# One ring of eight PSUM banks for layers three and four, and one tile for queries and values

## The chip, the cores and the metric

The kernel runs on one core of a Trainium2 chip. The metric is the device time of one execution in microseconds (us), lower is better. Engines are named as in the profile: PE is TensorE's matmul, PEld its weight load, DVE is VectorE, ACT is ScalarE, POOL is GpSimd, SP is SyncE, which issues all DMAs here.

## The reference

Two batches of eight heads, 768 positions, head size 64, all in float32. Attention over a window of 16 positions and over 24 block summaries gives a 1536 x 512 matrix `x`; two dense blocks follow.

```python
k_sum = k.reshape(B, H, nb, 32, D).max(axis=3); v_sum = v.reshape(B, H, nb, 32, D).mean(axis=3)
a = softmax(concat([where(|i - j| < 16, q k^T / 8, -1e9), q k_sum^T / 8 + log(32)]))
x = (a @ concat([v, v_sum])).transpose(...)                 # 1536 x 512
h = np.maximum(np.maximum(x @ w1, x @ w2), x @ w3)           # 1536 x 768  (layer one)
y = h @ moe_w_out                                            # 1536 x 512  (layer two)
out = ((y @ w_a) * (y @ w_b)) @ moe2_w_out                   # 1536 x 1536 (three), 1536 x 512 (four)
```

## The kernel before

The tokens are cut into four chunks of 384 (two to a batch). Attention is made group by group (a chunk and a pair of heads): queries `q_t` (four tiles taken in turn) and values `v_t` (one tile for each pair of heads) are loaded into SBUF, scores go to `ps`, transposed weights to `pst`, results to `psv`. Layers one and two (`layers12`) multiply weights by `x`, into PSUM tiles `ph` and `py`. Every float32 product is made of three fp32r matmuls (`mm3`: high by high, low by high, high by low part).

Layer three (`layer3`) is a seven-product scheme after Strassen and Winograd. For each of six pairs of column blocks `n` there is one pass of kind "a" and one of kind "b", and in a pass 7 products times two batches `b`. A product is 6 matmuls of 384 columns. The seven products of a batch use three PSUM banks, by the table `PRODUCTS`: products 0, 2, 4 and 6 add into bank `qb`, products 1 and 5 into bank `qg`, product 3 into `qd`. After each product the bank is read: products 0, 1 and 2 are copied by ACT (L626: `s`, `m`, `u`), 3, 4 and 5 are added to such a copy by DVE (L636 in kind "a", L642 in kind "b"), product 6 is read by ACT in kind "a" (L634) and by DVE in kind "b" (L640). So the read of product 6 is the last of `qb`, the read of product 5 the last of `qg`. Kind "b" goes on: POOL or DVE multiplies by the result of kind "a", and ACT and DVE split the product into `hg` (L514, L515).

Layer four (`layer4`) makes 12 output tiles for each `n`, 6 matmuls of 512 columns each into a bank `po`, three for each of two `hg`; ACT copies (`n` = 0) or DVE adds (L683) the bank to `acc`, which is stored at the last `n`. The order of the passes is a0, b0, a1, o0, b1, a2, o1 and so on (o is layer four); in the first and in the last pass of layer three all of batch 0 comes before batch 1.

Every PSUM tile belongs to a tag with a number of buffers. Before, `qb`, `qg` and `qd` have two each, and `po` shares the pair of tag `m` with layers one and two. The planner that builds the program places each tile in a bank, with no more tiles alive of a tag than its buffers, and orders the instructions of PE, ACT, DVE and POOL by its own cost model; each engine then runs its list in order. A tile in a bank that another held before waits for the last read of the other. SP's list stays in the order of the program text.

The weights of all layers come as 60 raw blocks (`w64`, 512 KB each, numbered q from 0) and are turned into float32 by ACT, DVE and POOL (`w_round`, L439 to L447), then split (`w_parts`, L451, L452). Blocks 0 to 7 have eight buffers of their own, blocks 8 to 23 (layers one and two) share `W64[0]` buffers, blocks 24 to 59 share `W64[1]` = 3. How far loads are written ahead of use depends on the same numbers:

```python
ahead = min(AHEAD[0] + 2 * (w_done < ERA0 + 4), W64[w_done + AHEAD[0] > N12] - 2 * (w_done >= ERA0 + 4))
```

with `AHEAD[0]` = 4, `ERA0` = 8, `N12` = 24, and `w_done` the count of blocks finished.

Of the kernel before, what the change touches and what calls it, by code (L numbers as in the profile page):

```python
# [9 lines left out]
F32 = mybir.dt.float32  # L10
# [8 lines left out]
B, H, S, D = 2, 8, 768, 64  # L19
P = 128  # L20
# [5 lines left out]
NP = H // 2  # L26
HALF = 64
WIN = HALF + 2 * WINDOW
NC = WIN + NB
# [7 lines left out]
NCH, MAXT = len(CHUNKS), max(SIZES)  # L37
# [5 lines left out]
N1, N2, NK = 3 * FF1 // P, FF1 // P, FF2 // P // 3  # L43
# [9 lines left out]

W64, W32, WBUFS, QB, FB, SM, GB, BANKS = (6, 3), (4, 3), (24, 10), 4, (9, 1), 2, (12, 9), (2, 2, 1, 2, 2)

GATE, ROOM, SUMS, EARLY34 = (2, 3), 16, (46, 48, 50, 52), 6
LEAD, TURN, ERA0, ASKS, AHEAD, PRE, TURNS = 5, (11, 2, 2), 8, (3, 4, 5, 7, 9), (4, 1), 3, ((6, N1 - 6, 6, 4, 4, 8, N1 - 8, 4, 12), (24, 34), (34, 44))

# [10 lines left out]
def attention_then_maxout_then_bilinear(ctx: ExitStack, tc: tile.TileContext, qt, kt, vt, vwin, wall, const, out):  # L77
# [6 lines left out]
    one = ctx.enter_context(tc.tile_pool(name="one", bufs=1))  # L84
# [14 lines left out]
    ps_m = ctx.enter_context(tc.tile_pool(name="ps_m", bufs=BANKS[3], space=PSUM))  # L99
# [9 lines left out]
    cst = take(C_ALL)  # L109
    ident = cst[:, C_ID:C_ID + P]  # L110

    q_t = [one.tile([P, MAXT, 2, P], F32, name=f"q{i}") for i in range(QB)]

    k_t = [take(NSEG * SEG) for _ in range(NP)]

    v_t = [one.tile([NC, MAXT, 2, 2, D], F32, name=f"v{p}") for p in range(NP)]
    VSEG, v_s = 2 * SIZES[0] + 1, {}


# [8 lines left out]
    marks, raw = {}, {}  # L130
# [3 lines left out]
    @contextmanager  # L134
    def behind_all(*names):

        with ExitStack() as held:
            for name in names:
                if name in marks:
                    held.enter_context(tc.issue_after(marks[name]))  # L140
            yield

    @contextmanager
    def chain(on=True):

        with behind_all("pe") if on else ExitStack():
            yield
# [89 lines left out]
    def scores(g, i):  # L237

        c, p = groups[g]
        t, q = CHUNKS[c][1] + i, q_t[g % QB]  # L240
        if i == 0:
            exps[g] = (sm_p.tile([P, MAXT, 2, NC], F32, tag="s", name="s"),
                       sm_p.tile([P, MAXT, 2], F32, tag="sm", name="sm"))
        s, sm = (x[:, i] for x in exps[g])
        ps = ps_s.tile([P, 2, NC], F32, tag="s", name="ps")
        nm = sm_p.tile([P, 2], F32, tag="nm", name="nm", bufs=4)
        with chain(g <= NP) if g <= NP else behind_all("first"):
            for a in range(2):
                k0 = (2 * t + a) * SEG + HALF - Z_AT[a]
                ins = T.matmul(ps[:, a], q[:, i, a], k_t[p][:, k0:k0 + NC], start=True, stop=True).ins  # L250
            if g <= NP:
                marks["pe"] = ins
        for a in range(2):
            mask = cst[:, MASK[t, a]:MASK[t, a] + NC]

            marks["scores", g, i] = V.tensor_tensor_reduce(s[:, a], ps[:, a], mask, -1.0 / D ** 0.5, 3e38, ALU.add, ALU.min, nm[:, a:a + 1]).ins  # L256
            A.activation(s[:, a], s[:, a], AF.Exp, bias=nm[:, a:a + 1], scale=-1.0, accum_out=sm[:, a:a + 1])  # L257
        if g <= NP:
            turn_over(TURN[1 + p // 2])
# [54 lines left out]
    def opening():  # L314

        def spread_(p, i):
            with behind_all(("scores", min(p + 1, NP - 1), i)):
                spread(0, p, raw["v", p])
# [178 lines left out]
    def flush():  # L497
        while late:
            late.pop(0)()

    def bank(name):

        return ps_m.tile([P, 512], F32, tag="m", name=name)
# [4 lines left out]
    def mm3(ps, w, o, x, first, last, more=False):  # L508

        for n, (i, j) in enumerate(((0, 0), (1, 0), (0, 1))):  # L510
            T.matmul(ps, w[:, i, o:o + P], x[:, j], start=first and n == 0, stop=last and n == 2, skip_group_check=more)  # L511

    def split(dst, src, eng):
        A.activation(dst[:, 0], src, AF.Copy)  # L514
        eng.tensor_tensor(dst[:, 1], src, dst[:, 0], ALU.subtract)  # L515
# [86 lines left out]
    def half(tag):  # L602
        return mo_p.tile([P, MAXT * P], F32, tag=tag, name=tag, bufs={"ca": 9, "t": 3}.get(tag, 2))

    def layer3(kind, n, cs):

        nonlocal w_freed
        ws = w_t[kind, n]
        ps, kept = {}, {}
        each = [(i, b) for i in range(7) for b in range(B)]  # L610
        if (kind, n) in (order34[0], order34[-2]):
            each.sort(key=lambda x: x[1])
        for i, b in each:
            w, y, bank_ = PRODUCTS[i]
            first = (b, bank_) not in ps
            if first:
                ps[b, bank_] = ps_m.tile([P, 512], F32, tag=f"q{bank_}", name=f"q{bank_}")[:, 0:MAXT * P]
            (wt, o), to = ws[w], ps[b, bank_]
            for k in range(2):
                mm3(to, wt, o + k * P, ops[b, y][:, :, k], first and k == 0, k == 1, not first)  # L620
            flush()

            def evac(i=i, b=b, to=to):
                def keep(name):
                    kept[b, name] = t = half(name)
                    A.activation(t, to, AF.Copy)  # L626

                def result(f, j, x):

                    c = 2 * b + j  # L630
                    if kind == "a":
                        cs[c, f] = t = half("ca")
                        if x is None:
                            A.activation(t, to, AF.Copy)  # L634
                        else:
                            V.tensor_tensor(t, to, x, ALU.add)  # L636
                        return
                    t = half("t")
                    if x is None:
                        V.tensor_tensor(t, to, cs[c, f], ALU.mult)  # L640
                    else:
                        V.tensor_tensor(t, to, x, ALU.add)  # L642
                        G.tensor_tensor(t, t, cs[c, f], ALU.mult)  # L643
                    gs[n, c, f] = g = hg_p.tile([P, 2, MAXT * P], F32R, tag="g", name="hg", bufs=GB[1])
                    split(g, t, V)

                if i in (0, 1, 2):
                    keep(("s1", "m5", "u2")[i])
                elif i == 3:
                    result(0, 0, kept[b, "s1"])  # L650
                elif i == 4:
                    result(1, 1, kept[b, "m5"])
                elif i == 5:
                    result(0, 1, kept[b, "u2"])
                else:
                    result(1, 0, None)

            late.append(evac)
            yield
        w_freed += 3  # L660
# [3 lines left out]
    def layer4(n, q):  # L664
        nonlocal w_freed
        for c in range(NCH):
            for i in range(CHUNKS[c][2]):
                ps = bank("po")
                for f in range(2):
                    w, g = w_t[q + f], gs[n, c, f][:, :, i * P:(i + 1) * P]  # L670
                    T.matmul(ps, g[:, 0], w[:, 0], start=(f == 0), stop=False)  # L671
                    T.matmul(ps, g[:, 0], w[:, 1], start=False, stop=False)  # L672
                    T.matmul(ps, g[:, 1], w[:, 0], start=False, stop=(f == 1))  # L673
                flush()

                def evac(c=c, i=i, ps=ps):
                    if n == 0:
                        if not acc:
                            sums = acc_p.tile([P, NCH, MAXT, DM], F32, tag="acc", name="acc", bufs=1)
                            acc.update({(c, i): sums[:, c, i] for c in range(NCH) for i in range(MAXT)})  # L680
                        A.activation(acc[c, i], ps, AF.Copy)
                    else:
                        V.tensor_tensor(acc[c, i], ps, acc[c, i], ALU.add)  # L683
                    if n == NG - 1:
                        r0 = (CHUNKS[c][0] * NT + CHUNKS[c][1] + i) * P
                        nc.sync.dma_start(out=out[r0:r0 + P, :], in_=acc[c, i])

                late.append(evac)
                yield
        w_freed += 2  # L690

    def layers34():
        q, cas = N12, {}
        for kind, n in order34:
            if kind == "o":
                flush()
                yield from layer4(n, q)
            else:
                yield from layer3(kind, n, cas.setdefault(n, {}))
            q += 2  # L700
# [99 lines left out]
```

## Time and profile before

| what | value |
|---|---|
| time, median of 3 runs | 561.99 us (561.78 to 562.42) |
| the profiled execution's own time | 562.49 us |
| its span, first to last instruction | 560.7 us |
| PE busy | 545.3 us, 97% of the span |
| DVE, ACT, POOL busy | 377.3, 279.2, 201.6 us |
| mean granted TensorE clock | 0.996 |

The profiled execution lies 0.5 us above the median; 1.8 us of its time lie outside the span. PE busy counts modelled ends of pipelined matmuls, so a busy PE is no proof of a PE at its peak; the idle times before its instructions are what can be won back.

### The profile page before, as it was taken

What the parts mean: (1) busy time and instruction counts of PE and PEld (TensorE: products, weight loads), DVE (VectorE), ACT (ScalarE), POOL (GpSimd) and SP (SyncE); (2) the same over time, 40 slices, a digit from 0 to 9 for tenths busy, and PEclk for the clock granted to TensorE, in tenths of its full rate; (3) what the DMA queues carried; (4) which work ended last, traced back from release to release, by engine and by line L of the source; (5) the groups of instructions that cost most, each with busy time, mean ns of one, the idle gap of its engine ahead of it and who ended that gap; (6) DMA issues with size and microseconds to landing.
All of it is one profiled execution on the core that took longest, in us unless ns stands there. A gap on an engine that the chain in (4) does not pass through costs nothing.

```text
span 560.7 us, 9032 instructions
## 1 busy us (share of the span) xinstructions
PE 545.3 (97%) x3374; PEld 516.3 (92%) x3374; DVE 377.3 (67%) x790; ACT 279.2 (50%) x672; POOL 201.6 (36%) x177
## 2 busy tenths in 40 slices
PE   8899999999999999999997999999999999999997
PEld 8889999999999999999997999999889989999985
DVE  5798966875323622739869756866967987773374
ACT  4799765766532413625675656534535443341220
POOL 3479997632010111513504322513412332220030
PEclk9999999999999999999999999999999999999999
DMA  8995244573000030313302222112023121000005
GB/s 302 367 304 227 79 150 147 180 221 100 22 1 1 2 111 3 113 38 114 113 0 77 75 76 75 44 69 85 29 76 113 37 77 38 1 0 1 1 33 192
DMA packets 16987, 51.81 MB, mean 92 GB/s; under 512 B 2096, under 2 KB 2480, under 8 KB 16944
## 3 DMA queue, kind: packets, MB, share of 16 engines
q1 hardware_dynamic: 16944, 51.25, 26.8%
q8 instruction: 26, 0.43, 0.3%
q14 instruction: 17, 0.14, 0.1%
HBM read 48.09 MB, written 3.15 MB: 91 GB/s over the span
## 4 chain that ended last, share of the span: by engine, by line
PE 79%; DVE 10%; DMA 5%; ACT 3%; issue 1%; POOL 1%; SPq 0%; ACTq 0%; DVEq 0%; POOLq 0%
PE ph L511 27%; PE qb L511 13%; PE py L511 9%; PE qg L511 6%; PE po L673 5%; PE po L672 5%; PE po L671 5%; PE ps L250 3%; PE qd L511 3%; DMA w<-wall 2%; DVE wt L452 2%; PE psv L305 2%; DVE hg L515 2%; PE pst L286 2%; DVE t L642 2%
## 5 line engine op out<-in xcount | busy, mean ns | idle before, releaser
L511 PE MATMUL ph<-x,wt 128*128 128x384 f32 x864 | 157.4, 337 | 0.0
L511 PEld LDWEIGHTS ph<-x,wt 128*128 128x128 f32 x864 | 149.0, 188 | 0.3
L447 POOL TENSOR_TENSOR w<-w,w 128x512 int32<-128x512 int32 x60 | 82.6, 1382 | 152.8 <-DVE w L446 90.1
L511 PE MATMUL qb<-yt,wt 128*128 128x384 f32 x576 | 113.9, 338 | 5.2 <-DVE t L642 3.1
L511 PEld LDWEIGHTS qb<-yt,wt 128*128 128x128 f32 x576 | 101.9, 188 | 10.7 <-DVE t L642 3.5
L514 ACT ACTIVATE hg<-t 128x384 fp32r<-128x384 f32 x72 | 37.0, 522 | 80.7 <-POOL t L643 34.3
L643 POOL TENSOR_TENSOR t<-t,ca 128x384 f32<-128x384 f32 x36 | 43.0, 1206 | 85.9 <-DVE t L642 85.9
L683 DVE TENSOR_TENSOR acc<-po,acc 128x512 f32<-128x512 f32 x60 | 40.8, 686 | 27.9 <-PE po L673 27.8
L511 PE MATMUL qg<-yt,wt 128*128 128x384 f32 x288 | 58.7, 340 | 0.5 <-DVE t L642 0.5
L671 PE MATMUL po<-wt,hg 128*128 128x512 f32 x144 | 56.2, 390 | 0.5 <-ACT hg L514 0.5
L672 PE MATMUL po<-wt,hg 128*128 128x512 f32 x144 | 56.7, 394 | 0.0
L673 PE MATMUL po<-wt,hg 128*128 128x512 f32 x144 | 56.2, 396 | 0.1
L511 PE MATMUL py<-hg,wt 128*128 128x384 f32 x288 | 54.7, 339 | 0.0
L511 PEld LDWEIGHTS qg<-yt,wt 128*128 128x128 f32 x288 | 51.9, 192 | 2.4 <-DVE t L642 0.8
L538 DVE TENSOR_TENSOR t<-ph,t 128x384 f32<-128x384 f32 x48 | 26.5, 554 | 37.3 <-PE ph L511 29.1
L511 PEld LDWEIGHTS py<-hg,wt 128*128 128x128 f32 x288 | 49.5, 188 | 0.2
L257 ACT ACTIVATE s<-s,nm 128x120 f32<-128x120 f32 x96 | 37.2, 392 | 22.1 <-DVE nm L256 21.7
L451 ACT ACTIVATE wt<-w 128x512 fp32r<-128x512 f32 (+1 forms) x60 | 35.1, 586 | 24.7 <-PE qb L511 15.3
L452 DVE TENSOR_TENSOR wt<-w,wt 128x512 fp32r<-128x512 f32 (+1 forms) x44 | 32.9, 748 | 18.6 <-ACT wt L451 18.5
L515 POOL TENSOR_TENSOR hg<-t,hg 128x384 fp32r<-128x384 f32 x24 | 26.8, 1121 | 46.4 <-ACT hg L514 46.4
L515 DVE TENSOR_TENSOR hg<-t,hg 128x384 fp32r<-128x384 f32 x48 | 40.8, 860 | 3.6 <-ACT hg L514 3.5
L443 ACT ACTIVATE w<-w 128x512 int32<-128x512 uint32 x60 | 39.0, 667 | 0.0
(80 smaller groups left out, 780.6 us busy)
## 6 DMA issues: line engine op xcount, KB each, us to landing
w<-wall SPq DMA_DIRECT2D x60, 512.0 KB, 3.4
q<-qt SPq DMA_DIRECT2D x15, 384.0 KB, 6.6
row<-kt SPq DMA_DIRECT2D x8, 416.0 KB, 5.0
full<-vt SPq DMA_DIRECT2D x8, 384.0 KB, 6.4
out<-acc SPq DMA_DIRECT2D x12, 256.0 KB, 2.0
v<-vwin SPq DMA_DIRECT2D x12, 192.0 KB, 6.0
v<-vwin SPq DMA_DIRECT2D x12, 96.0 KB, 5.6
q<-qt SPq DMA_DIRECT2D x1, 256.0 KB, 4.3
```

Source lines behind the costliest of these rows:

```text
L257: A.activation(s[:, a], s[:, a], AF.Exp, bias=nm[:, a:a + 1], scale=-1.0, accum_out=sm[:, a:a + 1])
L443: A.activation(lw.bitcast(I32), lw, AF.Copy, scale=2.0 ** -29)
L447: G.tensor_tensor(w.bitcast(I32), w.bitcast(I32), lw.bitcast(I32), ALU.add)
L452: eng.tensor_tensor(w[:, 1], r, w[:, 0], ALU.subtract)
L511: T.matmul(ps, w[:, i, o:o + P], x[:, j], start=first and n == 0, stop=last and n == 2, skip_group_check=more)
L514: A.activation(dst[:, 0], src, AF.Copy)
L515: eng.tensor_tensor(dst[:, 1], src, dst[:, 0], ALU.subtract)
L643: G.tensor_tensor(t, t, cs[c, f], ALU.mult)
L671: T.matmul(ps, g[:, 0], w[:, 0], start=(f == 0), stop=False)
L672: T.matmul(ps, g[:, 0], w[:, 1], start=False, stop=False)
L673: T.matmul(ps, g[:, 1], w[:, 0], start=False, stop=(f == 1))
L683: V.tensor_tensor(acc[c, i], ps, acc[c, i], ALU.add)
```

## The change

Layer three's three pairs and layer four's share of tag `m` become one tag `r` with eight buffers, so any of the tiles `qb`, `qg`, `qd` and `po` may take any free one of eight. The tag `m` keeps its pair for layers one and two. Queries and values become slices of one SBUF tile `held`. The buffers of weight blocks 8 to 23 go from six to four, which by the line quoted above also changes how far ahead these loads are written: from 6 to 4 blocks while `w_done` is under 12, and from 4 to 2 for `w_done` 12 to 20. The rename in `behind_all` has no effect on the program.

```diff
-W64, W32, WBUFS, QB, FB, SM, GB, BANKS = (6, 3), (4, 3), (24, 10), 4, (9, 1), 2, (12, 9), (2, 2, 1, 2, 2)
+W64, W32, WBUFS, QB, FB, SM, GB, BANKS = (4, 3), (4, 3), (24, 10), 4, (9, 1), 2, (12, 9), (2, 2, 1, 2, 2)
-LEAD, TURN, ERA0, ASKS, AHEAD, PRE, TURNS = 5, (11, 2, 2), 8, ...
+RING, LEAD, TURN, ERA0, ASKS, AHEAD, PRE, TURNS = 8, 5, (11, 2, 2), 8, ...
-    q_t = [one.tile([P, MAXT, 2, P], F32, name=f"q{i}") for i in range(QB)]
+    held = one.tile([P, QB + NP, MAXT, 2, P], F32, name="qv")
+    q_t = [held[:, i] for i in range(QB)]
-    v_t = [one.tile([NC, MAXT, 2, 2, D], F32, name=f"v{p}") for p in range(NP)]
+    v_t = [held[0:NC, QB + p].rearrange("k i a (h d) -> k i a h d", h=2) for p in range(NP)]
-        with ExitStack() as held:
+        with ExitStack() as pins:
-                ps[b, bank_] = ps_m.tile([P, 512], F32, tag=f"q{bank_}", name=f"q{bank_}")[:, 0:MAXT * P]
+                ps[b, bank_] = ps_m.tile([P, 512], F32, tag="r", name=f"q{bank_}", bufs=RING)[:, 0:MAXT * P]
-                ps = bank("po")
+                ps = ps_m.tile([P, 512], F32, tag="r", name="po", bufs=RING)
```

## Rows read from the trace of the kernel before

**Rows 1.** The page: busy time of each engine, its share, instructions.
```profile
PE 545.3 (97%) x3374; PEld 516.3 (92%) x3374; DVE 377.3 (67%) x790; ACT 279.2 (50%) x672; POOL 201.6 (36%) x177
```

**Rows 2.** Waits of PE alone: us in total, times, longest.
```profile
PE qb L511 <- DVE t L642: 3.1, 1, 3.1
...
PE qb L511 <- DVE t L640: 1.0, 3, 0.6
...
PE qb L511 <- ACT u L626: 0.6, 1, 0.6
PE qg L511 <- DVE t L642: 0.5, 1, 0.5
PE po L671 <- ACT hg L514: 0.5, 1, 0.5
PE qb L511 <- ACT s L626: 0.5, 1, 0.5
```

**Rows 3.** A window of 20 us: busy PE, PEld, DVE, ACT, POOL, PEclk, DMA share, GB/s.
```profile
300.00:320.00 20.00, 16.75 (x85) 15.81 (x84) 18.91 (x28) 12.46 (x25) 10.37 (x8) 0.91 0.28 98
```

**Rows 4.** Timeline around the longest wait: start, us, engine, instruction, [idle before <-releaser].
```profile
301.40 2.24 PE L511 MATMUL qb<-yt,wt 128*128 128x384 f32 x12
...
306.19 0.55 DVE L642 TENSOR_TENSOR t<-qb,m 128x384 f32<-128x384 f32 x1
306.65 0.54 DVE L642 TENSOR_TENSOR t<-qg,u 128x384 f32<-128x384 f32 x1
...
306.78 1.86 PE L511 MATMUL qb<-yt,wt 128*128 128x384 f32 x6 [3.14 <-DVE t L642]
```

**Rows 5.** Windows at that place, columns as in the window above.
```profile
303.50:306.70 3.20, 0.15 (x1) 0.00 (x0) 3.20 (x9) 2.59 (x5) 0.00 (x0) 1.00 0.04 12
...
307.40:310.60 3.20, 3.20 (x11) 3.20 (x11) 3.20 (x4) 1.36 (x3) 3.20 (x3) 0.50 0.24 60
```

**Rows 6.** Timeline of PE: two of four instructions that waited for a last read.
```profile
405.18 1.32 PE L511 MATMUL qb<-yt,wt 128*128 128x384 f32 x6 [0.57 <-DVE t L640]
451.57 1.34 PE L511 MATMUL qg<-yt,wt 128*128 128x384 f32 x6 [0.51 <-DVE t L642]
```

**Rows 7.** By tile, po: ns min/median/max, first and last start.
```profile
L671 PE MATMUL po<-wt,hg x144: 387/389/504, 287.9 to 556.0; 128*128 128x512 f32 x144
...
L681 ACT ACTIVATE acc<-po x12: 581/592/602, 317.9 to 348.5; 128x512 f32<-128x512 f32 x12
```

**Rows 8.** By tile, qd: the same columns.
```profile
L511 PE MATMUL qd<-yt,wt x144: 333/334/343, 244.9 to 508.7; 128*128 128x384 f32 x144
...
L642 DVE TENSOR_TENSOR t<-qd,s x12: 542/550/558, 269.8 to 539.8; 128x384 f32<-128x384 f32 x12
```

**Rows 9.** SP's timeline: issues of weight blocks 17 to 23, then of batch 1.
```profile
64.28 19.82 SPq L421 DMA_DIRECT2D w<-wall  x7
...
94.75 0.34 SPq L173 DMA_DIRECT2D full<-vt  x1
...
104.38 0.52 SPq L173 DMA_DIRECT2D full<-vt  x1
```

**Rows 10.** DMA issues of the weights: count, KB each, median us to landing.
```profile
w<-wall SPq DMA_DIRECT2D x60, 512.0 KB, 3.4
```

**Rows 11.** By line, L439: DVE's first step on every third early block, last on 22.
```profile
L439 DVE TENSOR_SCALAR psw<-w x8: 673/683/686, 28.3 to 98.7; 128x512 f32<-128x512 f32 x8
```

**Rows 12.** ACT's timeline: the first step on block 23.
```profile
101.36 0.62 ACT L441 ACTIVATE psw<-w 128x512 f32<-128x512 f32 x1
```

**Rows 13.** PE's timeline where layer two begins.
```profile
131.43 1.20 PE L511 MATMUL py<-hg,wt 128*128 128x384 f32 x6
```

**Rows 14.** The end, timeline: DVE's last read of a bank.
```profile
556.87 0.69 DVE L683 TENSOR_TENSOR acc<-po,acc 128x512 f32<-128x512 f32 x1 [0.67 <-PE po L673]
```

**Rows 15.** SP's timeline: a part of the tile `kept`, which also holds the keys.
```profile
3.54 0.43 SPq L224 DMA_DIRECT2D kept<-const  x1
```

**Rows 16.** Waits of POOL for what it writes into `kept`.
```profile
POOL kept L163 <- DMA row<-kt: 6.4, 2, 3.4
```

More of the change, by code (lines that the diff above doesn't have):

```diff
@@ L52 @@
             ("S4", "B22", "g"), ("A22", "T4", "b"))
-W64, W32, WBUFS, QB, FB, SM, GB, BANKS = (6, 3), (4, 3), (24, 10), 4, (9, 1), 2, (12, 9), (2, 2, 1, 2, 2)
+W64, W32, WBUFS, QB, FB, SM, GB, BANKS = (4, 3), (4, 3), (24, 10), 4, (9, 1), 2, (12, 9), (2, 2, 1, 2, 2)
 GATE, ROOM, SUMS, EARLY34 = (2, 3), 16, (46, 48, 50, 52), 6
-LEAD, TURN, ERA0, ASKS, AHEAD, PRE, TURNS = 5, (11, 2, 2), 8, (3, 4, 5, 7, 9), (4, 1), 3, ((6, N1 - 6, 6, 4, 4, 8, N1 - 8, 4, 12), (24, 34), (34, 44))
+RING, LEAD, TURN, ERA0, ASKS, AHEAD, PRE, TURNS = 8, 5, (11, 2, 2), 8, (3, 4, 5, 7, 9), (4, 1), 3, ((6, N1 - 6, 6, 4, 4, 8, N1 - 8, 4, 12), (24, 34), (34, 44))
 EARLY, BIAS_DVE, SPLIT_DVE = 16, ((0, 1, 0), (0, 1, 0), (0, 0, 0)), ((0, 0, 1), (0, 0, 1), (1, 1, 1))
@@ L135, in behind_all @@
     def behind_all(*names):
-        with ExitStack() as held:
+        with ExitStack() as pins:
             for name in names:
                 if name in marks:
-                    held.enter_context(tc.issue_after(marks[name]))
+                    pins.enter_context(tc.issue_after(marks[name]))
             yield
```

## Prediction

> **What bounds the kernel now.** I read the page first: PE is busy for 97% of the span and the next engine, DVE, for 67% [rows 1]. So only PE's idle time can be won, and the second view is the list of waits with PE as the waiting engine [rows 2]. Its rows that touch layers three and four are the six shown: 3.1 + 1.0 + 0.6 + 0.5 + 0.5 + 0.5 = 6.2 us. The third view is the windows: one of them, 300 to 320 us, holds half of that loss, and DVE is at 18.91 of 20 us there [rows 3]. The fourth is the timeline of that place [rows 4] and windows cut around it [rows 5]: PE stands still for 3.14 us, and right behind that the granted clock is 0.50 for 3.2 us and more, the lower of the two levels (1.2 GHz); before the wait it was 1.00. In the 20 us window the clock is 0.91, so the drop costs 0.09 x 20 = 1.8 us of full-speed work; the mean clock of the whole span, 0.996, leaves 0.004 x 560.7 = 2.2 us in all, so no other drop of that size is there. All in all layers three and four hold 6.2 + 1.8 = 8.0 us that any change of banks could give back. The end is no part of it: after PE's last matmul come DVE's last read of a bank at 556.87 us [rows 14] and the stores, with the same instructions in both kernels.
>
> **Ring of eight.** It removes no instruction and adds none: 576 + 288 + 144 matmuls of layer three, 432 of layer four, and their reads stay. What changes is which bank a tile may take. For each wait of [rows 2] I ask whether the releaser is the last reader of a bank. L640 reads product 6, the last of `qb`; so the three waits of `qb` for L640 (1.0 us together, the longest 0.57 [rows 6]) are first products of the next pass that wait for their pair. L642 on `qg` reads product 5, the last of `qg`; the wait of `qg` for it (0.5 us [rows 6]) is of the same kind. With eight banks to choose from the next pass can take another bank and these 1.0 + 0.5 = 1.5 us are free to go. The other waits are not for a free bank. `po` for ACT's `hg` (0.5 us) is data. `qb` for `u` and for `s` (0.6 and 0.5 us) is the next product that adds into a bank whose partial sum is still being copied. The wait of 3.14 us is of this kind too: the releaser at 306.19 reads `qb` with `m`, which only the read of product 4 does, and the six matmuls behind it are product 6, which adds into the same bank; nothing else stands between them and the 12 matmuls at 301.40 [rows 4]. A ring gives product 6 no other bank.
>
> Could the ring fill that wait with other work? PE runs its list in order; it would need the planner to have put groups of the next pass there. The total of banks does not grow: three pairs and a pair are eight, and so is the ring. At 303 us `qb` and `qg` banks are full and wait for DVE, which reads them from 306.19 and 306.65 on [rows 4], and `po` has held banks since 287.9 us, its first read being at 317.9 [rows 7]. So I take nothing for this wait. Bound of the gain from above: two groups of six matmuls (2.24 us for 12 [rows 4]) put in between leave 3.14 - 2.24 = 0.9 us; waits of 0.6 us and less leave the clock alone in this trace, so the drop would likely stay out as well: 2.24 + 1.8 = 4.0 us on top of the 1.5. Bound from below: 0.
>
> What the pairs protected is now shared. Products that need only early data are started long before they are read: the last `qd` starts by 508.7 us and the last read of a `qd` is at 539.8 [rows 8], the first `po` holds its bank for 30 us [rows 7]. With pairs such early starts could never hold more than two banks of `qd` and two of `po`; in the ring they may hold more and leave fewer to `qb` and `qg`. I price that in the rivals and take 0 for the likeliest case.
>
> **Waits that move to DVE or ACT.** If PE starts the next pass 0.5 us earlier at four places, the reads of that pass come earlier on engines at 67% and 50% [rows 1]. Cost 0, hidden by their idle time; without it, it is the wait just named.
>
> **W64 from six to four.** The buffers are taken by blocks 8 to 23. By the line that sets `ahead`, I counted the turns of the program: before, block 23 is written into SP's list at turn 22; after it, block 22 is at turn 26 and block 23 at turn 28. The loads of batch 1 begin in turn 24, and their second set in turn 25 to 26. So the DMA of block 22 moves behind `row`, `q`, `v`, `v` and `full`, whose last issue is at 94.75 us, and block 23 behind the second set, which ends at 104.38 + 0.52 us [rows 9]; before, all seven blocks 17 to 23 were issued by 84.1 us. With 3.4 us to landing [rows 10] block 22 lands at about 98.5 us; its first step on DVE is at 98.7 [rows 11]. Block 23 lands at about 108.3; its first step on ACT was at 101.36 [rows 12], so it comes 7 us late. What covers it: layer two, the first user of these blocks, starts on PE at 131.43 [rows 13], 23 us after that landing, for the six or so instructions that are left. Queued behind block 23 on ACT are the exponentials of batch 1, for which PE has layer-one matmuls to run meanwhile. I take 0; the bound is 7 us if PE's list has a score or a transpose at its head just then. Blocks 8 to 21 keep their order against all other loads, since no other load is written between them. Fewer buffers hold them back only until an earlier block is done, with two blocks of lead, 4.5 us of PE for each (12 matmuls of 2.24 us [rows 4], two chunks), against 3.4 us to landing; I take 0.
>
> **One tile for queries and values.** No instruction changes its size. It could cost if a load into one slice had to wait for reads of another. The kernel before has such a tile: masks and keys share `kept`, a load into it is issued at 3.54 us [rows 15], and POOL's write of keys into it waits for the key rows alone [rows 16]. So 0, with a bound of 0 below.
>
> **Sum.** 562.0 (the median; the profiled execution has 562.49, 0.5 more, of which 560.7 is span) - 1.5 = 560.5 us.
>
> **Rivals.**
> *The long wait goes too.* The planner, free of the pairs, puts a later group between products 4 and 6. For it: the next pass's first products need only `yt` and weights. Against: all eight banks are in use there. 562.0 - 1.5 - 4.0 = 556.5 us; with the last 1.6 us of small waits gone too, 554.9.
> *Nothing is won.* The order of all four engines is made anew, and the four waits come back elsewhere with the same size, since the chip's DVE runs later than the planned one (the 3.14 us show it): 562.0 us. The Trainium skill, "TensorE: Matmul & The Clock Gate", section "HAM oscillation — how this bites in real kernels", tells of a kernel in which PSUM double-buffering gave no further gain (126.6 to 125.5 us); by it the sum would be 562.0 as well. That trace was bound by other waits; here four waits do end at a last read, so I rank it second.
> *Slower: early starts fill the ring.* The mechanism is the one of [rows 7, 8]. A pass with one bank fewer must wait for a read between two products, as the 0.6 and 0.5 us of [rows 2] show, some 0.55 us each. One such wait in each of the 12 passes is 6.6 us: 562.0 - 1.5 + 6.6 = 567.1; in half of them 563.8. It decides from 5 such waits on (2.75 - 1.5 = 1.25 us slower).
> *Slower: block 23.* If ACT's wait reaches PE, up to 7 us: 562.0 - 1.5 + 7 = 567.5.
> *Slower: the clock.* In this trace the clock fell once, after 3.14 us of idle; the five kinds of wait of 0.6 us and less left it at 1.00. The skill's same page, section "A second HAM failure mode: psum-queue depth-cycling", says that cycling through PSUM banks leaves small pauses between groups of matmuls so often that the clock swings; by it a ring would cost, and at one drop of 1.8 us [rows 3] in each of 12 passes the time would be 562.0 + 21.6 = 583.6. The trace bears it out once, so I give it 2 in 100.
>
> **How the numbers follow.** Bank waits gone and nothing else: 0.34, with a range of its own from 559.5 to 561.5, mostly faster. The long wait too: 0.18, faster. Nothing won: 0.22, mostly the same. Early starts: 0.18. Block 23: 0.06. Clock: 0.02. A measurement here tells about 0.2%, 1.1 us, from no change. Faster: 0.26 of the first, 0.18, and 0.05 of nothing won, 0.49; same: 0.08 of the first, 0.13 of nothing won, 0.02 of early starts, 0.23; slower: the rest of nothing won, 0.04, of early starts, 0.16, block 23 and the clock, 0.28. The predicted time is the likeliest case's, 560.5. The range goes from the long wait's case, 556.0, to just under the full price of early starts, 566.0.
>
> **What would show it.** Right: among PE's waits no `qb` for L640 and no `qg` for L642; the wait of 3 us between products 4 and 6 still there near 300 us, with a clock of 0.50 behind it; weight blocks 22 and 23 issued near 95 and 105 us, PE full there. Wrong: PE waits for L626, L636 or L634 more than a dozen times (early starts); no wait of 3 us (the second case); idle PE between 95 and 135 us (block 23); several windows under 1.00 (the clock).

## The result, and the profile after

The changed kernel takes 555.88 us (median of 4 runs, 555.51 to 555.99) against 562.09 us before: 6.2 us less, ratio 0.989 with a 95% interval of 0.9878 to 0.9902. The prediction had the direction right and the size wrong: 560.5 us forecast, a gain of 1.5 us, and the measured time lies just below 556.0, the lower end of its range. One of the six executions of the ring of six (below) took 1378 us and is left out of its ratio.

The page of the changed kernel, busy times, to be read beside [rows 1]:

```profile
span 554.2 us, 9001 instructions
...
PE 541.0 (98%) x3374; PEld 514.9 (93%) x3374; DVE 372.7 (67%) x790; ACT 277.5 (50%) x672; POOL 202.0 (36%) x177
```

The same number of instructions on every engine, a span 6.5 us shorter. Helper lines stand one line lower in this kernel, so L643 here is L642 before, and so on. Its waits of PE, all that touch the layers from two on (engine, tile, line, releaser: us in total, times, longest):

```profile
PE py L512 <- ACT hg L515: 0.4, 1, 0.4
...
PE py L512 <- POOL hg L516: 0.2, 1, 0.2
PE qg L512 <- ACT m L627: 0.2, 1, 0.2
PE qb L512 <- ACT u L627: 0.2, 1, 0.2
```

Against the six rows of [rows 2], 6.2 us, layers three and four keep 0.2 + 0.2 = 0.4 us, and 0.6 us are new at the end of layer two. No product waits for L641 or L643 any more. The window that answers to [rows 3], same columns:

```profile
300.00:320.00 20.00, 20.00 (x112) 19.30 (x111) 19.95 (x35) 10.94 (x23) 8.38 (x6) 1.00 0.16 54
```

DVE is as full there as before, 19.95 of 20 us, and PE is full as well, at a granted clock of 1.00 where it was 0.91. The 1.8 us of the clock and 6.2 - 1.0 = 5.2 us of waits make 7.0 us. That this lies near the 6.5 us of span is partly luck, since two other terms nearly cancel. PE's last matmul ends 9.4 us earlier, at 547.4 instead of 556.8 us. Of the 2.4 us beyond the 7.0, layer four's matmuls show 1.7 in busy time (169.1 us before, 167.4 after); the cause was not looked into. Against it, the end behind the last matmul is 554.2 - 547.4 = 6.8 us long, where it was 560.7 - 556.8 = 3.9. The timelines of the end, before:

```profile
555.51 0.69 DVE L683 TENSOR_TENSOR acc<-po,acc 128x512 f32<-128x512 f32 x1 [0.67 <-PE po L673]
556.23 1.69 SPq L686 DMA_DIRECT2D out<-acc  x2
556.44 0.39 PE L673 MATMUL po<-wt,hg 128*128 128x512 f32 x1
```

and of the changed kernel:

```profile
546.35 2.48 DVE L684 TENSOR_TENSOR acc<-po,acc 128x512 f32<-128x512 f32 x4 [1.58 <-PE po L674]
547.05 0.39 PE L674 MATMUL po<-wt,hg 128*128 128x512 f32 x1
548.26 2.10 SPq L687 DMA_DIRECT2D out<-acc  x4
```

Before, the last adds to `acc` come 1.36 us apart (the last at 556.87 [rows 14]), each with its store behind it. In the changed kernel the last four stand together, and their four stores of 256 KB go out at once from 548.26 us on.

Where the wait of 3.14 us stood [rows 4], the timeline of PE, DVE and ACT now reads:

```profile
300.40 2.27 PE L512 MATMUL qb<-yt,wt 128*128 128x384 f32 x12
302.51 1.20 PE L512 MATMUL qg<-yt,wt 128*128 128x384 f32 x6
303.55 0.33 PE L512 MATMUL qb<-yt,wt 128*128 128x384 f32 x1
303.72 0.86 PE L512 MATMUL qg<-yt,wt 128*128 128x384 f32 x4
304.41 1.21 PE L512 MATMUL qb<-yt,wt 128*128 128x384 f32 x6
...
300.83 0.55 DVE L643 TENSOR_TENSOR t<-qb,m 128x384 f32<-128x384 f32 x1
...
305.40 0.54 DVE L641 TENSOR_TENSOR t<-qb,ca 128x384 f32<-128x384 f32 x1
...
307.93 0.54 DVE L641 TENSOR_TENSOR t<-qb,ca 128x384 f32<-128x384 f32 x1
...
302.94 0.47 ACT L627 ACTIVATE s<-qb 128x384 f32<-128x384 f32 x1
...
304.10 0.48 ACT L627 ACTIVATE m<-qg 128x384 f32<-128x384 f32 x1
```

Who reads a product tells which it is. The six matmuls at 304.41 last until 305.62, so the read at 305.40 is not theirs: they are the second batch's product 6, read at 307.93. Six of the 12 at 300.40 and all at 302.51 to 303.72 already belong to the next pass (its products 0 to 2); the copies `s` at 302.94 and `m` at 304.10 are the first reads of these. They fill the time in which DVE comes to read product 4 at 300.83, and they were started while the previous pass's product 6 had not been read (305.40 is the first such read). With pairs that was not allowed. By the reads four `qb` tiles are alive at 299 us: one whose product 6 is read at 300.17, the two read last at 305.40 and 307.93, and one of the next pass, copied at 297.97.

The early starts went the other way than the rival had it. By tile, po and then qd (ns min/median/max, first and last start):

```profile
L672 PE MATMUL po<-wt,hg x144: 387/389/398, 314.0 to 546.6; 128*128 128x512 f32 x144
```

```profile
L512 PE MATMUL qd<-yt,wt x144: 334/334/334, 245.1 to 525.4; 128*128 128x384 f32 x144
...
L643 DVE TENSOR_TENSOR t<-qd,s x12: 543/554/558, 292.9 to 532.5; 128x384 f32<-128x384 f32 x12
```

Layer four's first matmul comes at 314.0 instead of 287.9 [rows 7], and the last `qd` is held for at least 7 us (525.4 to 532.5) instead of 31 [rows 8]. Counted by products and reads, two `qd` and two `po` held banks at 303 us before; none does now. That the planner had started this work early because it had nothing better to place is a guess. Two runs below speak against a simple link: with three `qb` the wait of 3 us is gone though the first `po` still comes at 292.0 us, and with four `qg` a wait of 1.9 us stays though it comes at 309.9.

The weight blocks moved as foreseen. SP's timeline, for [rows 9]:

```profile
63.68 15.84 SPq L422 DMA_DIRECT2D w<-wall  x6
...
98.80 0.33 SPq L174 DMA_DIRECT2D full<-vt  x1
99.58 0.33 SPq L422 DMA_DIRECT2D w<-wall  x1
...
104.76 0.58 SPq L174 DMA_DIRECT2D full<-vt  x1
105.39 0.43 SPq L422 DMA_DIRECT2D w<-wall  x1
```

Block 22 is issued at 99.58 and block 23 at 105.39, each right behind the `full` of a set of batch 1. Their first steps come later than forecast (104.0 us on DVE and 111.3 on ACT, for 98.7 and 101.4 before), but PE is busy for all of 40 to 260 us in the windows, so it cost nothing there.

### The profile page after: what moved, and what is told of

It reads as the page before. It is cut to its first block, busy times and chain, and to the rows that moved or that the text cites. A ratio compares the mean times of both kernels' runs of the same rounds, so it can differ in the third digit from the quotient of the medians.

```text
span 554.2 us, 9001 instructions
## 1 busy us (share of the span) xinstructions
PE 541.0 (98%) x3374; PEld 514.9 (93%) x3374; DVE 372.7 (67%) x790; ACT 277.5 (50%) x672; POOL 202.0 (36%) x177
## 4 chain that ended last, share of the span: by engine, by line
PE 82%; DVE 5%; DMA 4%; ACT 3%; POOL 2%; issue 2%; SPq 0%; DVEq 0%; POOLq 0%; ACTq 0%
PE ph L512 24%; PE qb L512 15%; PE py L512 8%; PE qg L512 7%; PE po L673 5%; PE po L672 5%; PE po L674 5%; PE qd L512 4%; PE ps L251 3%; PE psv L306 2%; PE pst L287 2%; DVE wt L453 1%; DMA full<-vt 1%; DMA w<-wall 1%; DMA qv<-qt 1%
## 5 line engine op out<-in xcount | busy, mean ns | idle before, releaser
L512 PE MATMUL qb<-yt,wt 128*128 128x384 f32 x576 | 111.1, 336 | 0.2 <-ACT u L627 0.2
L644 POOL TENSOR_TENSOR t<-t,ca 128x384 f32<-128x384 f32 x36 | 44.6, 1253 | 70.3 <-DVE t L643 70.3
L673 PE MATMUL po<-wt,hg 128*128 128x512 f32 x144 | 56.2, 390 | 0.0
L672 PE MATMUL po<-wt,hg 128*128 128x512 f32 x144 | 56.1, 390 | 0.0
L674 PE MATMUL po<-wt,hg 128*128 128x512 f32 x144 | 55.1, 390 | 0.0
L684 DVE TENSOR_TENSOR acc<-po,acc 128x512 f32<-128x512 f32 x60 | 40.0, 684 | 19.6 <-PE po L674 19.6
L512 PEld LDWEIGHTS qg<-yt,wt 128*128 128x128 f32 x288 | 50.7, 188 | 0.6 <-ACT m L627 0.6
L442 ACT ACTIVATE w<-w 128x512 f32<-128x512 f32 x30 | 20.2, 673 | 46.0 <-DMA w<-wall 45.6
L516 DVE TENSOR_TENSOR hg<-t,hg 128x384 fp32r<-128x384 f32 x48 | 35.7, 756 | 5.4 <-ACT hg L515 5.2
```

## The experiments

**What makes room, without the ring.** The tile `held` and `W64[0]` = 4, PSUM tags as before:

```diff
-                ps[b, bank_] = ps_m.tile([P, 512], F32, tag="r", name=f"q{bank_}", bufs=RING)[:, 0:MAXT * P]
+                ps[b, bank_] = ps_m.tile([P, 512], F32, tag=f"q{bank_}", name=f"q{bank_}")[:, 0:MAXT * P]
-                ps = ps_m.tile([P, 512], F32, tag="r", name="po", bufs=RING)
+                ps = bank("po")
```

> Only what makes room for the ring: queries and values in one tile and four buffers in place of six for weight blocks 8 to 23; the three pairs and the pair stay. Theory (the banks made the gain): 562.1 us within 1.1, with PE waits of about 6 us in layers three and four again and a wait of about 3 us near 300 us. Rival (the new placing and order of loads made it, the ring none of it): 555.9 us within 1.1, PE waits there under 1.5 us.

Measured: 562.62 us against 561.96 of the kernel before on that chip, ratio 1.0012 (1.0001 to 1.0023). The waits of PE are those of [rows 2] again:

```profile
PE qb L512 <- DVE t L643: 3.1, 1, 3.1
PE qb L512 <- DVE t L641: 1.1, 3, 0.6
...
PE qg L512 <- DVE t L643: 0.6, 1, 0.6
PE qb L512 <- ACT u L627: 0.6, 1, 0.6
PE po L672 <- ACT hg L515: 0.5, 1, 0.5
```

So the whole gain comes with the banks, and with the order that the planner makes with them; the other edits cost about 0.1%.

**Layer four's banks alone.** As the last, but `po` has a tag of its own with eight buffers:

```diff
-                ps = bank("po")
+                ps = ps_m.tile([P, 512], F32, tag="o", name="po", bufs=RING)
```

> As the first kernel, but layer four's banks have eight buffers of their own and layer three keeps its three pairs. Theory (layer three's pairs are what held the order back): 562 us within 1.5. Rival (layer four's pair was what counted): near 556 us. A second rival, that more banks for early starts do harm: 564 us or more, with PE waits for the copies of layer three (ACT, s, m and u).

Measured: 564.31 us, ratio 1.0037 (1.0025 to 1.0049), with the 3.1 us wait of `qb` for L643 still there and waits of 1.2 us for L641. More banks for layer four don't help: 0.4% slower than before, 0.3% slower than the last kernel. The time is the one of the second rival, but not its reason: the waits for `u` are 0.6 us as before, and none for `s` or `m` is listed. What its trace shows is a longer end: PE's last matmul ends at 555.1 us, 2.2 us earlier than in the last kernel (557.4), but 6.5 us of the span follow it instead of 3.9, and the last four adds stand together as in the changed kernel.

**Pairs, in the order of the text.** As the first, and each product and each output tile is tied behind the one before on PE:

```diff
-            for k in range(2):
-                mm3(to, wt, o + k * P, ops[b, y][:, :, k], first and k == 0, k == 1, not first)
+            with behind_all("p34"):
+                for k in range(2):
+                    end = mm3(to, wt, o + k * P, ops[b, y][:, :, k], first and k == 0, k == 1, not first)
+            marks["p34"] = end
```

Layer four's loop gets the same four lines.

> As the first kernel (pairs), and the matmuls of layers three and four are tied to the order of the program text on PE, so nothing can be started early and nothing can fill a gap between two passes. Theory (the free banks themselves are needed): at each of some 11 passages from pass to pass, and in layer four, PE waits for the last reads of the pairs, 0.5 to 2 us each, so 565 to 585 us. Rival (only the order counts, early starts were the harm, pairs would do in the right order): 556 us within 1.5.

Measured: 598.04 us, ratio 1.064 (1.0602 to 1.0678), above the 585 us of the theory. Its waits of PE (here L644 is the read of product 6 in kind "b", L646 those of products 3 to 5):

```profile
PE qb L512 <- DVE t L644: 23.8, 5, 5.1
PE qb L512 <- DVE t L646: 5.7, 5, 1.4
```

And windows around one of the five, columns as in [rows 3]:

```profile
360.00:365.00 5.00, 1.31 (x6) 0.99 (x6) 5.00 (x7) 1.23 (x4) 4.64 (x4) 1.00 0.15 29
365.30:372.10 6.80, 5.33 (x17) 5.23 (x18) 5.60 (x9) 3.59 (x7) 1.97 (x2) 0.50 0.30 110
```

At the end of a pass of kind "b" the read of product 6 stands in DVE's list behind the splits of the other results and the weights' steps; DVE is busy for all of 360 to 365 us, in which PE does six matmuls and then stands. The wait is 23.8 / 5 = 4.8 us, not the 0.5 to 2 us expected, and the granted clock is 0.50 from 365.3 to 372.1.

**The ring, in the order of the text.** The changed kernel with the same tie:

```diff
+            with behind_all("p34"):
...
+            marks["p34"] = end
```

> The changed kernel with the same tie to the order of the program text. Theory and rival alike: with eight banks the text's order costs little, 555.9 to 558 us; the distance to the third kernel is what the banks are worth at one and the same order. If it is as slow as the third kernel, the gain lies in the free order on PE that the ring allows, not in the wait for banks.

Measured: 570.39 us, ratio 1.0144 (1.0113 to 1.0175). The waits for the read of product 6 in kind "b" are gone from the list; those for L646, product 6 behind product 4 in the same bank, stay at 5.9 us in 5 waits, as in the third kernel. So at one and the same order the banks are worth 598.0 - 570.4 = 27.7 us, and the free order on PE is worth 570.4 - 555.9 = 14.5 us more. The two stand in for each other: with pairs the free order is worth 598.0 - 562.6 = 35.4 us, and in the free order the banks are worth 562.6 - 555.9 = 6.7. The ring without the free order is slower than the kernel before. My expectation that the text's order would cost next to nothing was wrong.

**Layer three alone in the ring.** `po` on the pair of tag `m` (`GB[1]` 8 for 9 to make room):

```diff
-                ps = ps_m.tile([P, 512], F32, tag="r", name="po", bufs=RING)
+                ps = bank("po")
```

> The ring of eight for layer three's tiles alone; layer four goes back to the pair of tag m (and its split tiles hg have eight buffers in place of nine, to make room). Theory (layer three's pairs held the order back): 555.9 us within 1.5, PE waits in layers three and four under 2 us. Rival (one ring for both layers is needed, since layer four's tiles have to wait in line with layer three's): 560 us or more.

Measured: 555.46 us, ratio 0.9884 (0.9865 to 0.9903). All of the gain, though `po` now waits for the reads of its pair (1.4 us in 3 waits for L684).

**Four buffers for qb alone.** No ring, pairs for the others (`WBUFS[1]` 9 for 10 to make room):

```diff
-... tag="r", name=f"q{bank_}", bufs=RING)[:, 0:MAXT * P]
+... tag=f"q{bank_}", name=f"q{bank_}", bufs=4 if bank_ == "b" else 2)[:, 0:MAXT * P]
```

> No ring: bank qb has four buffers, qg, qd and layer four's keep their pairs (and nine weight tiles of layers three and four in place of ten, to make room). Theory in its narrow form (only qb's pair stops the next pass, since its last read is product 6): 556 us within 1.5 and no PE wait of 3 us. Rival (qg is needed too, since the next pass goes on with product 1): 559 to 562 us, with waits of qg for the read of product 5.

Measured: 555.16 us, ratio 0.9884 (0.9867 to 0.9901). All of the gain from two more `qb`, without any `qg` wait for the read of product 5. The waits of PE from layer three on:

```profile
PE qg L512 <- ACT m L627: 1.1, 1, 1.1
...
PE qb L512 <- ACT u L627: 0.4, 1, 0.4
...
PE qb L512 <- DVE t L641: 0.2, 1, 0.2
```

**Four of each, no common ring.**

```diff
-... tag="r", name=f"q{bank_}", bufs=RING)[:, 0:MAXT * P]
+... tag=f"q{bank_}", name=f"q{bank_}", bufs=4)[:, 0:MAXT * P]
-                ps = ps_m.tile([P, 512], F32, tag="r", name="po", bufs=RING)
+                ps = ps_m.tile([P, 512], F32, tag="o", name="po", bufs=4)
```

> No common ring: qb, qg, qd and po have four buffers each of their own, 16 in name, and the eight banks are shared by the planner as before. Theory (what counts is that two of a kind is lifted, not that the tiles share one tag): 555.9 us within 1.5. Rival (sharing counts, without it early starts fill the banks): 560 us or more with PE waits for the copies of layer three.

Measured: 555.44 us, ratio 0.9886 (0.9869 to 0.9903). Sharing one tag is not what counts.

**A ring of six.**

```diff
-RING, LEAD, TURN, ERA0, ASKS, AHEAD, PRE, TURNS = 8, 5, ...
+RING, LEAD, TURN, ERA0, ASKS, AHEAD, PRE, TURNS = 6, 5, ...
```

> The changed kernel with a ring of six in place of eight: just the six banks that one pass of layer three uses. Theory: the next pass finds a bank once qd and qg are read, so most of the gain stays, 556 to 559 us. Rival (the gain needs whole spare banks beside a pass): 562 us or more, with waits of qb for the last reads and a wait of 3 us again.

Measured: 560.17 us, ratio 0.9969 (0.9957 to 0.9982). A quarter of the gain, between the two expectations: the 3 us wait is gone, but `qg` waits 2.7 us in three waits for L643 instead: a first product still finds no bank until an old one is read. PE's last matmul ends 4.4 us earlier than in the kernel before; a longer end (5.8 us) takes 2.0 of that back.

**Three buffers for qb.** The room is that of the changed kernel, `po` is on the pair of tag `m`, so against the first of these kernels one buffer is all that differs:

```diff
-... tag="r", name=f"q{bank_}", bufs=RING)[:, 0:MAXT * P]
+... tag=f"q{bank_}", name=f"q{bank_}", bufs=3 if bank_ == "b" else 2)[:, 0:MAXT * P]
```

> The changed kernel without the ring: one buffer more for qb (three), pairs for qg, qd and layer four. Theory (a spare qb bank lets the next pass begin before product 6 is read): one spare serves one of two batches, so most or all of the gain, 555.5 to 558 us, and the wait of 3 us gone. Rival (two spares, one for each batch, are needed): 559 us or more.

Measured: 557.55 us, ratio 0.9915 (0.9895 to 0.9935): about three quarters of the gain (0.85 of 1.1%) from one spare bank, and no wait above 0.9 us for layer three. Layer four's first matmul is at 292.0 us here, and two `qd` hold banks at 303 us as before, so early starts alone are not what made the long wait.

**Four for qg, and four for qd,** `qb` back to its pair, else as the last:

```diff
-... bufs=3 if bank_ == "b" else 2)[:, 0:MAXT * P]
+... bufs=4 if bank_ == "g" else 2)[:, 0:MAXT * P]      # and "d" in the other kernel
```

> As the one before, but qb keeps its pair and qg has four. Theory (only qb's last read comes late enough to matter): 562 us or more, since more early products of qg fill banks and order nothing better; the wait of 3 us stays. Rival (any two more banks do, since it is the order that is loosened): 557 us or less.

> The same with qd: four for qd, pairs for the others. Theory: 562 us within 1.5, the wait of 3 us stays. Rival: 557 us or less.

Measured: 563.74 us, ratio 1.0034 (1.0023 to 1.0045), and 568.51 us, ratio 1.0116 (1.0098 to 1.0135). Both are slower than before, though with four `qg` the first `po` comes later (309.9 us). The waits of PE with four `qd`, the larger ones:

```profile
PE qb L512 <- DVE t L643: 2.9, 1, 2.9
PE qb L512 <- DVE ca L637: 2.3, 2, 1.4
PE qg L512 <- DVE t L643: 2.3, 1, 2.3
```

The wait of `qb` for the read of product 4 stays in both (1.9 and 2.9 us), as the theory had it. That the kernel with four `qd` would lose 1.2% it had not; the new waits are those of product 6 for the read of product 4 in kind "a" (2.3 us) and of `qg` for the read of product 5 (2.3 us), but why the planner's order gets worse with more `qd` is not settled.

**One ring for all dense layers.** Layers one and two draw from the ring too (`W64[0]` 3 to make room):

```diff
-        return ps_m.tile([P, 512], F32, tag="m", name=name)
+        return ps_m.tile([P, 512], F32, tag="r", name=name, bufs=RING)
```

> The ring taken further: layers one and two draw from the same eight banks as three and four (and three buffers in place of four for weight blocks 8 to 23, to make room). What is left of PE's waits in the changed kernel is about 1 us where layer two ends and 0.4 us in layer three, so the theory allows at most 1.5 us: 554.4 to 556.5 us. Rival (layers one and two gain from more than two banks): 553.5 us or less.

Measured: 557.16 us, ratio 0.9914 (0.9897 to 0.9931): above the 554.4 to 556.5 us expected, and no better than the change itself; the rival fails too. None of the variants is clearly faster than the change: `qb` with four, four of each and layer three alone have ratios of 0.9884 to 0.9886, within the interval of its 0.989.

## Why the prediction was right or wrong

*What could be won* was right for the 8.0 us of waits and lost clock: 7.0 of them came back. It was wrong on the end, which it left out because the instructions are the same. They are, but their order is not, and the end grew by 2.9 us; layer four's faster matmuls (1.7 us) were not foreseen either. The forecast has neither term, and they nearly cancel.

*The four waits for a last read* (1.5 us) went, as predicted: no wait for L641 or for `qg`'s L643 is left.

*The long wait* is the step that failed. I took nothing for it, on the argument that product 6 gets no other bank from a ring and that all eight banks are in use there, so nothing could be put in between. The first half holds: the wait for product 4's read is still there as a wait when the text's order is kept (5.7 us with pairs, 5.9 us with the ring). The second half was wrong. All eight banks were indeed taken at 303 us, but this was read off a plan that had been made under the pairs. Not the total of eight stopped the next pass, but the count of two for `qb`: with three the gain is 0.85%, with four 1.2%, and more buffers for any other kind alone are no gain. Given a third `qb`, products of the next pass stand between product 4 and product 6, and the 3.1 us and the 1.8 us of clock behind it go together: 4.9 us where I took 0. My upper bound for this, 4.0 us, was also low: it left 0.9 us of the wait, and none is left. The chance for this case, 0.18, was too small. Its own sum is 556.5 us; for the 556.0 us at which the range begins there is no working.

*The small waits in one bank* (0.6 and 0.5 us) and for `hg` (0.5 us) I had as staying. The changed kernel lists 0.2 us for `u`, none for `s` and none for `po` on `hg`, and 0.2 us for `m`; that the freer order covers them is likely, but was not tested alone. Against it stand 0.6 us of new waits for `hg` at the end of layer two.

*Early starts fill the ring* did not happen in the changed kernel; first `po` and last `qd` come later than before. More buffers for `qg`, `qd` or `po` without more for `qb` do lose (0.3%, 1.2%, 0.4%), so a loss of that size exists, though for other tiles. For `po` the trace shows it at the end, not in waits; for `qg` and `qd` that early starts are the cause was not shown.

*W64 and the common tile* at 0 were right within 0.1%: the kernel with these alone is at 1.0012, and the two late blocks were issued right behind the sets of batch 1, 4.6 and 0.4 us from the times named.

*The clock.* The Trainium skill, "TensorE: Matmul & The Clock Gate", section "A second HAM failure mode: psum-queue depth-cycling", tells of a kernel that cycles through PSUM banks and whose clock swings for the small pauses this leaves; read as a rule it would have the ring swing the clock. The row of the changed kernel shows 1.00 where it was 0.91, so here fewer waits meant a steadier clock. The kernel with pairs in the text's order shows the other side, 0.50 with each wait of 5 us. The same page of the Trainium skill, section "HAM oscillation — how this bites in real kernels", tells of double-buffering in PSUM that gave no further gain. Here the step from two to three banks of one tile gave 0.85%, so the measurement differs, since here a last read did end PE's waits.

## What to carry to other kernels

Ask which PSUM tile is read last in a pass, and how long its read stands behind other work on its engine: that tile needs banks for the next pass before any other does. Here one spare gave three quarters of what a common ring of eight gave, and two gave all of it. A bank that looks taken in a planned program may be free under another limit: the plan was made under the limits that it has. A wait inside one bank is not fixed either: spare banks of its kind let other groups stand in front of it. And look at the end as well as at the waits: more banks for the last output tiles let their adds and stores come all at once, which here cost 2 to 3 us.

## What the runs showed that was not expected

A read that is last in a pass can be late by 4.8 us on an engine that is busy for 65% of that run's span: DVE's list was full from 360 to 365 us around one of them. DVE's split of `hg` (128x384) took 860 ns on the mean before and 756 ns in the changed kernel, the same 48 instructions, 35.7 us in place of 40.8; this was not looked into. The clock mostly follows long waits: in the kernel with pairs in the text's order, 36.1 us slower than the kernel before, the two rows of waits are 29.5 us, and a stretch at 0.50 goes with each of the five long ones. But the length of the wait alone does not decide it: in the trace of layer four's banks alone the clock stays at 1.00 behind the wait of 3.1 us, and with four `qg` it is 0.51 from 310.0 to 313.5 us, behind a wait of 1.9 us. The windows, of the one and then of the other, columns as in [rows 3]:

```profile
300.00:320.00 20.00, 15.82 (x83) 14.13 (x83) 19.47 (x29) 11.90 (x25) 10.87 (x8) 1.00 0.30 106
```

```profile
310.00:313.50 3.50, 3.50 (x12) 3.10 (x11) 3.46 (x4) 1.67 (x4) 3.48 (x3) 0.51 0.00 0
```

The mean clock of the kernel before goes from 0.994 to 1.000 between executions, so its drop is not the same each time.

The end behind PE's last matmul has two sizes. It is 5.8 to 6.8 us in the four kernels in which `po` may take six or eight banks in free order (the change, layer four's banks alone, the ring of six, one ring for all), and 3.8 to 3.9 us in the ten others, the ring in the text's order and layer three alone in the ring among them. In those four the last four or five adds stand together.
